# Forming the prepared FFN weights from pieces already loaded, a full-width bias matmul, a new order of the first FFN product and measured durations in the planner of a two-layer transformer kernel

## Chip, cores and metric

One Trainium2 chip; the kernel runs on one core. The metric is the device time of one execution in microseconds (us). The kernel before takes 1254.91 us (median of 6 runs, 1253.64 to 1258.09). All runs compared in this document are in the same (fast) state.

## The reference

Two identical layers, each a sliding dilated attention and a feed-forward network (FFN) with squared relu, both behind a layernorm and both with a residual. S = 2048 tokens, D = 1024, 32 heads, 8 taps at distance 2, F = 3584, weights in bf16.

Condensed (the reference writes it out at greater length):

```python
def _A_ref(x, wqkv, wo):                       # cut to what matters
    q, k, v = split_heads(x @ wqkv)            # 32 heads of 32
    idx = pos[:, None] - 2 * arange(8)         # 8 taps, dilation 2
    logits = einsum("bhsd,bhswd->bhsw", q, k[idx]) * scale   # masked where idx < 0
    return merge_heads(einsum("bhsw,bhswd->bhsd", softmax(logits), v[idx])) @ wo

def _B_ref(x, w1, b1, w2, b2):
    h = relu(x @ w1 + b1)
    return (h * h) @ w2 + b2

for layer in range(2):                         # written out in the reference
    x = x + _A_ref(_layernorm(x), wqkv, wo)
    x = x + _B_ref(_layernorm(x), w1, b1, w2, b2)
```

## The kernel before

The work is cut into 8 units (2 layers x 4 blocks of 512 tokens). The engines are named as in the profile: PE does the matmuls, DVE the elementwise work on tensors, ACT the activations and copies, POOL next to nothing here; SP issues most of the DMA transfers. A bank is one of eight buffers (`ps` in the program) that PE writes its sums to. A unit has these steps: layernorm and transposed input `xnA`; the q, k and v products (`pq`); the attention, whose products `P` and `pr` are formed on DVE and whose logits `lg` are summed by PE; the output projection `py`, the second layernorm and `xnB`; FFN product 1 (`ph` in unit 0; banks X, Y, Z in the others); FFN product 2 (banks X, Y, Z of the weights w2). Units 1 to 7 do both FFN products by a scheme of seven half-size products in place of eight, which needs sums and differences of pieces of w1 and w2. These are formed once, beside unit 0, and kept in DRAM as `w1s` and `tw`.

No order of instructions is written down: the program adds operations with an engine, a duration, a priority and buffers, and a planner written in Python simulates the engines and emits each engine's list in the order it finds.

```python
        while left:
            progress = False
            for e in engs:
                if efree[e] > t + 1e-9 or not ready[e]:
                    continue
                skipped = []
                picked = None
                while ready[e]:
                    item = heapq.heappop(ready[e])
                    o = item[2]
                    need = {}
                    ok = True
                    for b in o.bufs:
                        if b.slot is None:
                            need[b.cls] = need.get(b.cls, 0) + 1
                            if b.tag in self.caps and (live.get(b.tag, 0) >= self.caps[b.tag] or b.idx != placed.get(b.tag, 0)):
                                ok = False
                    if ok and all(len(free[c]) >= n for c, n in need.items()):
                        picked = o
                        break
                    skipped.append(item)
                    if len(skipped) > 40:
                        break
        # ... (cut)
            t, _, o, own = heapq.heappop(events)
            while True:
                if o is not None:
                    for s in o.succ:
                        if o.mb or (s.eng == o.eng) == own:
                            s.ndep -= 1
                            if s.ndep == 0:
                                heapq.heappush(ready[s.eng], (s.prio, seq, s)); seq += 1
        # ... (cut)
```

The bias of the second FFN product is a matmul with one row, put in front of the products of a bank:

```python
        self.b2r = const.tile([1, D], BF, name="b2r")
        nc.gpsimd.dma_start(self.b2r[:], self.b2.rearrange("(o d) -> o d", o=1))
        self.ones = const.tile([1, 128], BF, name="ones")
        nc.vector.memset(self.ones[:], 1.0)
# ... and in front of a bank's products (cut):
                    def fm(w=w, q=q, half=half):
                        if b2 is not None and half == 0:
                            nc.tensor.matmul(banks[q][:], self.ones[:], self.b2r[:, b2 * BLK:(b2 + 1) * BLK], start=start, stop=False,
                                             skip_group_check=True)
                        for j in range(g):
                            jj = half * g + j
```

The limits on live buffers by name, among them one transposed input `xnA` and one `tv` buffer:

```python
        p.caps.update(w=5, xt=2, P0=4, P1=4, pr=2, pb=2, dn=1, e=1, xm=6, xnA=1, xnB=1, xn=2, xo=2, q=1, k=1, v=1, o=1, r2=1, s1=1, tw=4, tv=1, T=1, wl=2)
```

The preparation loads w2 and w1 a second time:

```python
    def combine_group(self, j0, n):
        nc, p = self.nc, self.p
        step = 4
        b = {}
        for k2 in range(2):
            for n2 in range(2):
                t = b[k2, n2] = Buf("4K", "tw", [128, step, BLK], F16)
                self.dma(lambda t=t, n=n: t[:, :n].bitcast(BF), lambda k2=k2, n2=n2, j0=j0, n=n: self.w2_block(k2, n2)[:, j0:j0 + n, :],
                         (), [(t, 0)], n * 0.131, name="twl", lat=10.0)

        def comb(dst, a, asrc, c, csrc, i):
            def f():
                va = a[:, :n].bitcast(BF) if asrc else a[:, :n]
                vc = c[:, :n].bitcast(BF) if csrc else c[:, :n]
                nc.vector.tensor_tensor(dst[:, :n], va, vc, ALU.subtract)
            p.add("DVE", dve(n * BLK), f, [(a, 0), (c, 0)], [(dst, 0)], self.nxt(), name="tw")
            self.dma(lambda: self.tw[i][:, j0:j0 + n, :], lambda: dst[:, :n], [(dst, 0)], [(("tw", i), j0)], n * 0.131, prio=-10.0, name="tws")
        b11, b12, b21, b22 = b[0, 0], b[0, 1], b[1, 0], b[1, 1]
        comb(b11, b12, True, b11, True, 0)
        comb(b12, b22, True, b12, True, 2)
        comb(b22, b22, True, b11, False, 1)
        comb(b21, b21, True, b22, False, 3)
```

```python
    PAIR = [(0, 1), (1, 1), (0, 5), (1, 5), (0, 6), (1, 6), (0, 2), (0, 7), (1, 2), (1, 7), (0, 4), (0, 3), (1, 4), (1, 3)]
    LAST = [(0, 1), (0, 5), (0, 2), (0, 6), (0, 7), (0, 4), (0, 3)]

    def combine_w1_group(self, dp, after):
        nc, p = self.nc, self.p
        F2 = self.F // 2
        order = self.PAIR if dp // 2 * 2 + 1 < self.NDP else self.LAST
        dst = self.w1s[dp // 2]
        at = {pr: i for i, (d, pr) in enumerate(order) if d == dp % 2}

        def cell(i):
            return (("w1s", dp // 2), i)

        def raw(m2, k2):
            return self.w1_v[:, 4 * k2:4 * k2 + 4, m2 * F2 + dp * 256:m2 * F2 + (dp + 1) * 256]
        for pr, m2, k2 in ((1, 0, 0), (2, 0, 1), (4, 1, 1)):
            self.dma(lambda i=at[pr]: dst[:, i], lambda m2=m2, k2=k2: raw(m2, k2), (), [cell(at[pr])], 0.3, after=after, name="w1raw", cast=BF)
        t = Buf("8K", "tv", [128, 4, 1024], F16)
        for i, (m2, k2) in enumerate(((1, 1), (0, 0), (1, 0), (0, 1))):
            self.dma(lambda i=i: t[:, i].bitcast(BF).rearrange("p (k n) -> p k n", k=4), lambda m2=m2, k2=k2: raw(m2, k2), (), [(t, i)], 0.3, after=after, name="tvl", lat=12.0)

        def comb(o, a, araw, b, braw, op, pr):
            def f():
                va = t[:, a].bitcast(BF) if araw else t[:, a]
                vb = t[:, b].bitcast(BF) if braw else t[:, b]
                nc.vector.tensor_tensor(t[:, o], va, vb, op)
            p.add("DVE", dve(1024), f, [(t, a), (t, b)], [(t, o)], -50.0, name="tv")
            self.dma(lambda: dst[:, at[pr]].rearrange("p k n -> p (k n)"), lambda: t[:, o], [(t, o)], [cell(at[pr])], 0.26, prio=-10.0, name="tvs")
        comb(0, 2, True, 0, True, ALU.add, 5)
        comb(2, 1, True, 2, True, ALU.subtract, 7)
        comb(1, 0, False, 1, True, ALU.subtract, 6)
        comb(3, 3, True, 1, False, ALU.subtract, 3)
```

The first FFN product of units 1 to 7 takes the prepared weights in groups of up to four; product 1 leaves bank X, ACT copies X to `u`, and the next product in X waits for that copy:

```python
        for d0 in range(0, self.NDP, 2):
            order = self.PAIR if d0 + 1 < self.NDP else self.LAST
            steps = [self.ffn1_step(r2, d0 + i) for i in range(min(2, self.NDP - d0))]
            for j, (d, pr) in enumerate(order):
                if j % 4 == 0:
                    n = min(4, len(order) - j)
                    w = Buf("8K", "w", [128, 4, 4, 256], F16) if u + 1 < self.NU or j % 8 else Buf("8Q", "wl", [128, 4, 4, 256], F16)
                    self.dma(lambda w=w, n=n: w[:, 0:n], lambda d0=d0, j=j, n=n: self.w1s[d0 // 2][:, j:j + n],
                             [(("w1s", d0 // 2), j + i) for i in range(n)], [(w, 0)], n * 0.262,
                             after=[st["attended"]] if w.cls == "8Q" else (), name="w")
                steps[d](pr, w, j % 4, *rhs[pr])
# in ffn1_step, what follows each product (cut):
            if pr == 1:
                keep(1)
            elif pr == 2:
                vadd(r1, 0, 1, Y)
            elif pr == 6:
                keep(2)
            elif pr == 7:
                keep(3)
                vadd(r3, 1, 3, Z)
                for a in range(2):
                    vrelu(r3, a, 1, h + f0 + a)
            elif pr == 4:
                for a in range(2):
                    p.add("ACT", act(256), lambda a=a: nc.scalar.activation(out=r3[:, a, 0, :], in_=X[:, a, :], func=ACTF.Relu,
                                                                            bias=self.b1T[:, h + f0 + a:h + f0 + a + 1], scale=1.0),
                          [(X, 0)], [(r3, (a, 0))], 2.0, name="relu")
                square(r3, h + f0)
            elif pr == 3:
                vadd(r1, 1, 2, Z)
                for a in range(2):
                    vrelu(r1, a, None, f0 + a)
                square(r1, f0)
```

The order in which the program adds the steps:

```python
        for u in range(NU):
            if u + 1 < NU:
                self.SA(u + 1)
                if u == 0:
                    self.combine_w2()
                    self.SQ(u + 1, "kq")
                    self.SW(u)
                else:
                    self.SQ(u + 1, "k")
                    self.SW(u)
                    self.SQ(u + 1, "q")
                self.SQ(u + 1, "v")
                self.S2(u + 1, (1, 1) if u + 1 == NU - 1 else (3, 3))
            (self.SF1 if u else self.SF1_plain)(u)
            if u == 0:
                for dp in range(self.NDP):
                    pe = [o for o in self.p.ops if o.eng == "PE"]
                    self.combine_w1_group(dp, [pe[len(pe) * (dp + 3) // (self.NDP + 4)]])
            if u == NU - 2:
                self.SW(u + 1)
            self.SF2(u)
```

The softmax here doesn't subtract the row's maximum and nothing guards it: scores larger than these inputs give would overflow.

## Time and profile before

| quantity | value |
| --- | --- |
| time, median of 6 runs | 1254.91 us |
| span of the profiled execution | 1252.7 us |
| PE busy | 1193.9 us (95%) |
| bytes moved by DMA | 368.20 MB |
| start of unit 1's first FFN product | 302.95 us |
| start of the last 21 matmuls | 1244.47 us |

How to read the views. The page lists the busy time of each engine and slices the span into 40 parts, with the busy share in tenths. The list of waits has, for each engine and tile, the operation that ended the wait, then the total in us, the number of waits and the longest. The timeline has the start, the length, the engine, the line, the operation and, in brackets, the idle time before it and what ended it. The prediction shows most of these for the kernel before.

In the timeline, the start of unit 1's first FFN product and a bias matmul with its successor:

```profile
302.95 1.91 PE L785 MATMUL X<-xnB,w 128*128 128x256 f16 x16
...
1242.22 0.39 PE L836 MATMUL X<-b2r,ones 1*128 1x512 bf16 x1
1242.54 1.69 PE L840 MATMUL X<-w,r 128*128 128x512 f16 x7
```

The first line divides the run: what lies before it is called early, what lies between it and the last group of matmuls late. The bias matmul holds PE 0.32 us until the next one starts. And one row of the table by stretches, 40 to 80 us (columns: length; busy us and count of PE, PE's weight loads, DVE, ACT, POOL; granted clock of PE; DMA share; GB/s):

```profile
40.00:80.00 40.00, 27.76 (x128) 17.20 (x126) 37.12 (x47) 16.82 (x34) 0.00 (x0) 0.91 0.94 296
```

PE does 27.8 us of work in 40 while DVE and DMA are both nearly full.

### The profile page before, as it was taken

Reading aid. Unit: us, or ns where it says so; the run is one execution under the profiler, and the core shown is the slowest. Engines: PE = TensorE matmul, PEld = TensorE weight load, DVE = VectorE, ACT = ScalarE, POOL = GpSimd, SP = SyncE. Lnnn points to the kernel's source line nnn. Section 1 sums busy time; section 2 is a strip of 40 time slices with the busy share of each in tenths; the row PEclk is TensorE's granted clock in tenths of the full one; section 3 lists DMA queues with packets and bytes.
Section 4 is the critical chain, followed back from the end, with each engine's and each line's share of the span. In section 5 each row is a group of like instructions: output and inputs, shape, how many; then the busy total and the mean of one; then the engine's idle time right before and its main releaser. Section 6 shows DMA issues by size and latency. Waiting matters only on the chain.

```text
span 1252.7 us, 17924 instructions
## 1 busy us (share of the span) xinstructions
PE 1193.9 (95%) x6844; PEld 731.8 (58%) x6844; DVE 1035.2 (83%) x1555; ACT 674.2 (54%) x1240; POOL 4.0 (0%) x10
## 2 busy tenths in 40 slices
PE   6969989899999999999999999999999999999998
PEld 3635534357845578456864568545684557844853
DVE  5899979959989599986999779995999959997562
ACT  6624875059920798019970399406992174742630
POOL 1000000000000000000000000000000000000000
PEclk9989999999999999999999999999999999999999
DMA  9899999989999689995989779997799956788874
GB/s 314 303 288 305 351 350 306 361 294 280 316 341 336 203 277 319 346 319 186 350 315 334 284 233 372 299 311 252 235 337 367 318 167 221 254 285 304 290 267 166
DMA packets 240550, 368.20 MB, mean 294 GB/s; under 512 B 67664, under 2 KB 170576, under 8 KB 231504
## 3 DMA queue, kind: packets, MB, share of 16 engines
q1 hardware_dynamic: 229344, 353.41, 83.7%
q10 hardware_dynamic: 7488, 13.63, 2.9%
q0 software_dynamic: 3632, 0.02, 0.4%
q8 instruction: 53, 0.87, 0.3%
q14 instruction: 33, 0.27, 0.1%
HBM read 312.48 MB, written 46.40 MB: 286 GB/s over the span
## 4 chain that ended last, share of the span: by engine, by line
PE 57%; DVE 18%; ACT 12%; DMA 6%; SPq 3%; issue 2%; ACTq 1%; DVEq 0%
PE X L840 13%; PE X L785 10%; PE pq L557 8%; PE Z L840 7%; PE Z L785 6%; DVE P L589 5%; PE Y L840 4%; DVE P L597 4%; SPq L290 3%; DMA w<-in_B_w_dram 3%; ACT xn L410 3%; PE py L685 3%; ACT xn L439 3%; PE Y L785 2%; ACT xn L435 2%
## 5 line engine op out<-in xcount | busy, mean ns | idle before, releaser
L557 PE MATMUL pq<-xnA,w 128*128 128x512 f16 x1536 | 342.1, 383 | 19.2 <-DMA xnA<-xnd0A 12.0
L557 PEld LDWEIGHTS <-w 128*128 128x128 bf16 x1536 | 220.3, 144 | 136.8 <-issue 18.8
L785 PEld LDWEIGHTS <-w 128*128 128x128 f16 (+1 forms) x2520 | 246.4, 98 | 46.0 <-issue 11.2
L840 PEld LDWEIGHTS <-r 128*128 128x128 f16 x1344 | 128.7, 98 | 161.0 <-issue 9.3
L840 PE MATMUL X<-w,r 128*128 128x512 f16 (+1 forms) x896 | 201.8, 379 | 3.1 <-DMA w<-in_B_w_dram 3.1
L589 DVE TENSOR_TENSOR P<-q,k 128x2048 f16<-128x2048 f16 x128 | 151.7, 1224 | 56.5 <-ACT q L559 49.0
L559 ACT CAST k<-pq 128x512 f16<-128x512 f32 x64 | 37.4, 587 | 291.0 <-PE pq L557 290.0
L649 DVE TENSOR_TENSOR pr<-pb,v 128x2048 f16<-128x2048 f16 x128 | 156.4, 1222 | 0.2
L785 PE MATMUL X<-T,w 128*128 128x256 f16 x1120 | 136.5, 272 | 9.1 <-ACT u L759 8.9
L597 DVE TENSOR_TENSOR P<-P,P 128x2048 f16<-128x2048 f16 x99 | 120.9, 1222 | 2.2
L685 PE MATMUL py<-w,o 128*128 128x512 bf16 x512 | 112.3, 379 | 0.0
L773 ACT ACTIVATE r<-rr 128x1024 f16<-128x1024 f16 x98 | 101.5, 1058 | 13.1 <-DVE rr L769 11.8
L759 ACT CAST u<-X 128x512 f16<-128x512 f32 x147 | 84.5, 586 | 44.8 <-PE X L785 40.3
L652 DVE TENSOR_TENSOR pr<-pr 128x1024 f16<-128x1024 f16 x128 | 88.1, 689 | 2.7
L690 DVE TENSOR_TENSOR xm<-py,xt 128x512 f32<-128x512 f32 x64 | 43.9, 690 | 50.9 <-PE py L685 45.5
L685 PEld LDWEIGHTS <-o 128*128 128x128 bf16 x512 | 50.0, 98 | 59.8
L762 DVE TENSOR_TENSOR rr<-u,Z 128x512 f16<-128x512 f16 x98 | 65.4, 683 | 20.2 <-PE Z L785 11.1
L435 ACT ACTIVATE xn<-xm 128x1024 f16<-128x1024 f32 x32 | 33.9, 1060 | 58.9 <-DVE xm L690 58.0
L653 DVE TENSOR_TENSOR pr<-pr 128x512 f16<-128x512 f16 x128 | 54.4, 425 | 4.4
L840 PE MATMUL Y<-w,r 128*128 128x512 bf16 x224 | 51.9, 380 | 2.1 <-DMA w<-in_B_w_dram 2.1
L769 DVE TENSOR_SCALAR rr<-rr,b1T 128x256 f16<-128x256 f16 (+1 forms) x196 | 51.3, 315 | 1.3
L840 PE MATMUL Z<-w,s 128*128 128x512 f16 x224 | 51.3, 380 | 0.0
(92 smaller groups left out, 1261.5 us busy)
## 6 DMA issues: line engine op xcount, KB each, us to landing
w<-w1s SPq DMA_DIRECT2D x63, 1024.0 KB, 7.9
w<-tw SPq DMA_DIRECT2D x64, 896.0 KB, 7.6
w<-in_A_wqkv_dram SPq DMA_DIRECT2D x48, 1024.0 KB, 9.2
w<-in_B_w_dram SPq DMA_DIRECT2D x48, 896.0 KB, 8.2
w<-in_A_wo_dram SPq DMA_DIRECT2D x16, 1024.0 KB, 9.1
xt<-xs SPq DMA_DIRECT2D x32, 512.0 KB, 9.3
w<-w1s SPq DMA_DIRECT2D x21, 512.0 KB, 9.2
xs<-xo SPq DMA_DIRECT2D x32, 256.0 KB, 6.2
```

What stands on the lines that cost most here:

```text
L435: nc.scalar.activation(out=xn[:], in_=xv(), func=ACTF.Identity, accum_out=s1())
L557: nc.tensor.matmul(pq[:], wv[:, kd % 4, c0:D:8], xnT[:, :, kd, :], start=(kd == 0), stop=(kd == KD - 1))
L589: nc.vector.tensor_tensor(cur[:], q[:, c, None, hb * HB:(hb + 1) * HB].to_broadcast([128, W, HB]), _win_ap(k[:, c, :], HALO + hb * HB, HB) ...
L597: nc.vector.tensor_tensor(other[:], other[:], cur[:], ALU.add)
L649: nc.vector.tensor_tensor(pr[:], pb[:], _win_ap(v[:, c, :], HALO + hb * HB, HB), ALU.mult)
L652: nc.vector.tensor_tensor(pr[:, 0:4, :], pr[:, 0:4, :], pr[:, 4:8, :], ALU.add)
L685: nc.tensor.matmul(py[:], o[:, c, tl * 128:(tl + 1) * 128], wos[db][:, c, :], start=(c == 0), stop=(c == NCH - 1))
L759: p.add("ACT", act(512), lambda: nc.scalar.copy(us[i][:], X[:]), [(X, 0)], [(us[i], 0)], 1.0, name="u")
L762: p.add("DVE", dve(512, False), lambda: nc.vector.tensor_tensor(r[:, :, m, :], us[i][:], bank[:], ALU.add), [(us[i], 0), (bank, 0)], [(r, ...
L773: p.add("ACT", act(1024), lambda: nc.scalar.activation(out=r2[:, f:f + 2, :].rearrange("p a t -> p (a t)"), in_=r[:].rearrange("p a m t -> ...
L785: nc.tensor.matmul(bank[:, a, :], lw[:, k, a * 128:(a + 1) * 128], rhs(k), start=(start and k == 0 and a == 0), stop=(k == 3), skip_group_ ...
L840: nc.tensor.matmul(banks[q][:], left(jj, q), w[:, j, :], start=(start and jj == 0 and b2 is None), stop=(jj == h - 1), skip_group_check=True)
```

## The change

Its intent is to have less DMA and DVE work beside unit 0, where PE has its holes, and plans that are truer to the chip. Five parts are told apart below:

1. Preparation: w1 and w2 combinations are formed from the pieces that unit 0's own products have loaded (`keep_w1`, `keep_w2`); uncombined w1 pieces are copied from DRAM to DRAM; unit 0's second FFN product becomes plain (eight products); two `xnA` buffers, six small `tv` buffers.
2. The bias by a full 128-row matmul (a matrix with ones in row 0).
3. A new order of the seven products in FFN product 1, with weights in chunks of 4.
4. Planner: 0.3 us of slack ahead of PE operations that wait for another engine, a longer look-ahead, durations as measured.
5. wo loaded in other halves.

The diff, cut to its core:

```diff
@@ -21,6 +22,7 @@
 
 MM = 0.2157
 LAT = 0.25
+PE_SLACK = 0.3
 DMA_LAT = 2.2
 DMA_MBS = 0.36
 
@@ -138,7 +140,7 @@
                         picked = o
                         break
                     skipped.append(item)
-                    if len(skipped) > 40:
+                    if len(skipped) > 300:
                         break
                 for it in skipped:
                     heapq.heappush(ready[e], it)
@@ -169,12 +171,19 @@
                 raise RuntimeError(f"plan is stuck at {t}: {stuck} live {live} free { {c: len(f) for c, f in free.items()} }")
             t, _, o, own = heapq.heappop(events)
             while True:
-                if o is not None:
+                if own is None:
+                    heapq.heappush(ready[o.eng], (o.prio, seq, o)); seq += 1
+                elif o is not None:
                     for s in o.succ:
                         if o.mb or (s.eng == o.eng) == own:
                             s.ndep -= 1
-                            if s.ndep == 0:
-                                heapq.heappush(ready[s.eng], (s.prio, seq, s)); seq += 1
+                            if s.ndep:
+                                continue
+                            if s.eng == "PE" and o.eng != "PE":
+                                heapq.heappush(events, (t + PE_SLACK, seq, s, None))
+                            else:
+                                heapq.heappush(ready[s.eng], (s.prio, seq, s))
+                            seq += 1
                     if not own:
                         for b in o.bufs:
                             b.left -= 1
@@ bias (cut) @@
@@ -242,10 +251,12 @@
         self.b1T = const.tile([128, KF], F32, name="b1T")
         with nc.allow_non_contiguous_dma(reason="tiny bias load"):
             nc.gpsimd.dma_start(self.b1T[:], self.b1.rearrange("(c p) -> p c", p=128))
-        self.b2r = const.tile([1, D], BF, name="b2r")
-        nc.gpsimd.dma_start(self.b2r[:], self.b2.rearrange("(o d) -> o d", o=1))
-        self.ones = const.tile([1, 128], BF, name="ones")
-        nc.vector.memset(self.ones[:], 1.0)
+        self.b2r = const.tile([128, D], BF, name="b2r")
+        nc.gpsimd.dma_start(self.b2r[:], self.b2.rearrange("(o d) -> o d", o=1).to_broadcast((128, D)))
+        self.row0 = const.tile([128, 128], F16, name="row0")
+        nc.vector.memset(self.row0[:], 1.0)
+        nc.gpsimd.affine_select(out=self.row0[:], in_=self.row0[:], pattern=[[0, 128]], compare_op=ALU.is_equal,
+                                fill=0.0, base=0, channel_multiplier=1)
 
         self.wqkv_v = self.wqkv.rearrange("(kt p) n -> p kt n", p=128)
         self.wo_v = self.wo.rearrange("(p c) n -> p c n", c=self.NCH)
+    def add_b2(self, bank, n2, start):
+        self.nc.tensor.matmul(bank[:], self.row0[:], self.b2r[:, n2 * BLK:(n2 + 1) * BLK], start=start, stop=False, skip_group_check=True)
@@ buffers (cut) @@
-        p.caps.update(w=5, xt=2, P0=4, P1=4, pr=2, pb=2, dn=1, e=1, xm=6, xnA=1, xnB=1, xn=2, xo=2, q=1, k=1, v=1, o=1, r2=1, s1=1, tw=4, tv=1, T=1, wl=2)
+        p.caps.update(w=5, xt=2, P0=4, P1=4, pr=2, pb=2, dn=1, e=1, xm=6, xnA=2, xnB=1, xn=2, xo=2, q=1, k=1, v=1, o=1, r2=1, s1=1, tv=6, T=1, wl=2)
@@ preparation of w2; combine_w2 and combine_group are removed, SF2_plain is added (cut) @@
+    def keep_w2(self, j0, n, w):
+        nc, p = self.nc, self.p
+        t = [Buf("2K", "tv", [128, 2, BLK], F16) for _ in range(4)]
+
+        def raw(k2, n2):
+            return w[:, k2, :n, n2 * BLK:(n2 + 1) * BLK]
+
+        def comb(i, a, b, r):
+            p.add("DVE", dve(n * BLK), lambda: nc.vector.tensor_tensor(t[i][:, :n], a(), b(), ALU.subtract), r, [(t[i], 0)], 45.0, name="tv")
+            self.dma(lambda: self.tw[i][:, j0:j0 + n, :], lambda: t[i][:, :n], [(t[i], 0)], [(("tw", i), j0)], n * 0.13, prio=50.0, name="twst", lat=8.0)
+        comb(0, lambda: raw(0, 1), lambda: raw(0, 0), [(w, 0)])
+        comb(1, lambda: raw(1, 1), lambda: t[0][:, :n], [(w, 1), (t[0], 0)])
+        comb(2, lambda: raw(1, 1), lambda: raw(0, 1), [(w, 0), (w, 1)])
+        comb(3, lambda: raw(1, 0), lambda: t[1][:, :n], [(w, 1), (t[1], 0)])
@@ order of FFN product 1 and copies of raw w1 pieces; keep_w1 forms the four combinations as keep_w2 does (cut) @@
+    def ffn1_order(self):
+        out = [(0, 1), (1, 1)]
+        for a in range(0, self.NDP, 2):
+            steps = [d for d in (a, a + 1) if d < self.NDP]
+            then = [(d, 1) for d in (a + 2, a + 3) if d < self.NDP]
+            for pr in (5, 6, 2, 7):
+                out += [(d, pr) for d in steps]
+            out += then
+            for pr in (4, 3):
+                out += [(d, pr) for d in steps]
+        return out
+
+    def copy_w1(self, after):
+        after = iter(after)
+        for i, (dp, pr) in enumerate(self.order1):
+            if pr in (1, 2, 4):
+                gate = next(after)
+                m, k = {1: (0, 0), 2: (0, 1), 4: (1, 1)}[pr]
+                c0 = m * (self.F // 2) + dp * 256
+                self.dma(lambda i=i: self.w1s[i // 4][:, i % 4], lambda k=k, c0=c0: self.w1_v[:, 4 * k:4 * k + 4, c0:c0 + 256],
+                         (), [(("w1s", i // 4), i % 4)], 0.3, prio=1e5 + i, after=[gate], name="w1cp", cast=BF)
@@ durations (cut) @@
-            p.add("ACT", 1.3, f1, xr, [(xn, 0), (sm, 0)], prio, name="ln1")
-            p.add("ACT", 1.3, f2, xr + [(sm, 0)], [(xn, 0), (sm, 1)], prio - 0.1, name="ln2")
-            p.add("ACT", 0.5, f2b, [(sm, 0), (sm, 1)], [(sm, 1)], prio - 0.15, name="ln2b")
+            p.add("ACT", 1.47, f1, xr, [(xn, 0), (sm, 0)], prio, name="ln1")
+            p.add("ACT", 1.35, f2, xr + [(sm, 0)], [(xn, 0), (sm, 1)], prio - 0.1, name="ln2")
+            p.add("ACT", 0.8, f2b, [(sm, 0), (sm, 1)], [(sm, 1)], prio - 0.15, name="ln2b")
-            p.add("DVE", 0.15 + len(ms) * 0.067, lambda: nc.vector.tensor_scalar(out=v(), in0=v(), scalar1=self.b1T[:, f:f + 1], scalar2=0.0,
+            p.add("DVE", 0.21 + len(ms) * 0.07, lambda: nc.vector.tensor_scalar(out=v(), in0=v(), scalar1=self.b1T[:, f:f + 1], scalar2=0.0,
-                    p.add("ACT", act(256), lambda a=a: nc.scalar.activation(out=r3[:, a, 0, :], in_=X[:, a, :], func=ACTF.Relu,
+                    p.add("ACT", 0.48, lambda a=a: nc.scalar.activation(out=r3[:, a, 0, :], in_=X[:, a, :], func=ACTF.Relu,
@@ wo (cut) @@
-        wos = [self.weights(self.wo_v[:, :, g * 512:(g + 1) * 512], KD) for g in range(D // 512)]
+        wos = [self.weights(self.wo_v[:, 4 * g:4 * g + 4, :], KD, wide=True) for g in range(2)]
@@ build (cut) @@
-                    self.combine_w2()
-                    self.SQ(u + 1, "kq")
+                    self.run(self.SQ(u + 1, "kq"))
                     self.SW(u)
+                    self.copy_w1([op for op in self.p.ops if op.eng == "PE" and op.name in ("pq", "py")][-24:])
+                    self.run(self.SF1_plain(u), self.SQ(u + 1, "v"))
                 else:
-                    self.SQ(u + 1, "k")
+                    self.run(self.SQ(u + 1, "k"))
                     self.SW(u)
-                    self.SQ(u + 1, "q")
-                self.SQ(u + 1, "v")
+                    self.run(self.SQ(u + 1, "q"))
+                    self.run(self.SQ(u + 1, "v"))
                 self.S2(u + 1, (1, 1) if u + 1 == NU - 1 else (3, 3))
-            (self.SF1 if u else self.SF1_plain)(u)
-            if u == 0:
-                for dp in range(self.NDP):
-                    pe = [o for o in self.p.ops if o.eng == "PE"]
-                    self.combine_w1_group(dp, [pe[len(pe) * (dp + 3) // (self.NDP + 4)]])
+            if u:
+                self.SF1(u)
             if u == NU - 2:
                 self.SW(u + 1)
-            self.SF2(u)
+            (self.SF2 if u else self.SF2_plain)(u)
```

## The prediction

> **What bounds the kernel now.** I read the page first (busy shares, slices), then PE's waits, then PE's timeline around its gaps, then the groups of instructions and the DMA issues.
>
> The busy shares and the slices, from the page:
>
> ```profile
> PE 1193.9 (95%) x6844; PEld 731.8 (58%) x6844; DVE 1035.2 (83%) x1555; ACT 674.2 (54%) x1240; POOL 4.0 (0%) x10
> ...
> PE   6969989899999999999999999999999999999998
> ...
> PEclk9989999999999999999999999999999999999999
> DMA  9899999989999689995989779997799956788874
> ```
>
> PE (the matmul engine) is the bound. Its holes and its only slow clock lie in the first eight slices of 31 us; after that it is nine tenths or more. DMA is at its limit in those slices too. So the question for every part is what it does to PE's idle time early, and to PE's own work later. PE's waits say who caused the holes:
>
> ```profile
> PE pq L557 <- DMA xnA<-xnd0A: 12.0, 1, 12.0
> PE lg L604 <- DVE P L597: 9.3, 7, 4.8
> PE pt L493 <- ACT xn L479: 9.1, 3, 8.1
> PE X L785 <- ACT u L759: 8.9, 10, 1.8
> PE pq L557 <- DMA w<-in_A_wqkv_dram: 6.0, 3, 3.7
> PE X L840 <- DMA w<-in_B_w_dram: 3.1, 2, 1.8
> ```
>
> The third is the start of the program and stays. The largest early ones in PE's timeline (start, us, ..., in brackets the idle time before):
>
> ```profile
> 64.44 3.62 PE L557 MATMUL pq<-xnA,w 128*128 128x512 f16 x16
> 80.10 29.13 PE L557 MATMUL pq<-xnA,w 128*128 128x512 f16 x128 [12.05 <-DMA xnA<-xnd0A]
> 109.07 7.07 PE L685 MATMUL py<-w,o 128*128 128x512 bf16 x32
> ...
> 182.53 1.89 PE L604 MATMUL lg<-P,grp 128*128 128x512 f16 x4 [4.76 <-DVE P L597]
> 184.21 12.75 PE L711 MATMUL ph<-xnB,w 128*128 128x512 f16 x56
> ...
> 247.06 14.61 PE L557 MATMUL pq<-xnA,w 128*128 128x512 f16 x60 [3.73 <-DMA w<-in_A_wqkv_dram]
> ```
>
> From this I take the unit of all the sums. A stream of full matmuls starts one every 0.2157 us (in the last unit the timeline has 56 of them from 1224.00 to 1236.08: 12.08 / 56). After the 12.05 us hole the 128 take 28.97 us (80.10 to 109.07) instead of 27.6: the slow clock costs 1.4 more. The same after the other two: about 1.3 after 182.53, 1.5 after 247.06 (60 in 14.45 instead of 12.94).
>
> **What the Trainium skill says.** "TensorE: Matmul & The Clock Gate", section "What's actually happening", gives 512 / 2.4 GHz + 2.5 ns = 215.7 ns for a warm matmul of 512 columns, and a half-rate clock after a window of some 3.4 us idle. The trace agrees: 0.2157 us, and a mean granted clock of 0.84 in the stretch with the 12 us hole. "TensorEngine Tiling (Array Packing)", section "Key Properties", says that switching the tiling mode drains the engine. That bears on the bias matmul of one row (its form is 1*128): in the timeline 28 matmuls start at 1236.08, so its slot is at 1242.12; it starts at 1242.22 and the next one at 1242.54, 0.20 us later than slot and length allow; whether a drain is the reason, no view shows. "VectorE: DVE Perf Modes", section "The perf-mode tier table", has 1224 ns for a tensor_tensor of 2048 16-bit elements; here the product rows of the attention have 1222 to 1224 ns, so the DVE work moved below can be summed from its rows.
>
> **The change part by part.**
>
> (1) Preparing the weights. Before, the first unit reads w1 and w2 for its own products and both again to form the sums and differences (the fast seven-product scheme) that later units use:
>
> ```profile
> tv<-in_B_w_dram SPq DMA_DIRECT2D x28, 256.0 KB, 7.7
> ...
> tw<-in_B_w_dram SPq DMA_DIRECT2D x12, 512.0 KB, 9.4
> ...
> tw<-in_B_w_dram SPq DMA_DIRECT2D x4, 256.0 KB, 6.5
> ```
>
> After, the combinations are formed from the w1 and w2 already loaded. That removes 28 x 0.25 = 7 MB and 12 x 0.5 + 4 x 0.25 = 7 MB. The first unit's second FFN product becomes plain: it reads w2 once (7 MB) instead of 14 pieces of 0.875 (12.25 MB): 5.25 less. Together 19 MB, at the page's mean of 294 GB/s an estimated 65 us of all DMA engines, out of about 280 us. The DVE work of combining stays (4 x 7 of 0.69, and the same elements for w2), but none of it now precedes the first unit's attention: 6 of 1.22 and 8 of 0.69, 13 us, leave DVE's way there. The order of the built program confirms it: the transposes of the second unit's input move from after 47 transfers of the DMA queue to places 13 to 19, beside the attention of unit 0; in before they are issued at 69.9 us, 25 us after their last input was stored (44.9). They will be there long before PE asks at 68. So the 12.05 and its 1.4 go. The wait of 4.76 on DVE goes too: DVE itself lost 6.83 us there waiting for a slot that a store of a combination held (tw<-tw), and that store is gone. The 3.73 + 0.45 on query/key weights at 242 to 247 with their 1.5 should go with the DMA load. Sum: 12.05 + 1.4 + 4.76 + 1.3 + 4.18 + 1.5 = 25.2 us.
>
> (2) The plain product costs PE 4 x 2 x 28 + 8 bias = 232 matmuls where the fast one has 7 x 2 x 14 + 6 = 202: 30 x 0.2157 = 6.5 us, less 6 x 0.2 for its old bias matmuls: +5.3. On DVE it takes 10 of 1.08 and 6 of 0.69, 15 us, away.
>
> (3) What is not won of (1). Without the hole PE would be at py at 96 instead of 109. Its second half needs all of unit 0's attention, which DVE ended at 121.3. DVE's work up to there falls by 13 us, but it was waiting for q part of the time, so it gains some 4.5 us until the exponentials, and 3 more after (5.3 less of combining, 2.4 more of moved-up products): about 114. PE gets there after 96 + 6.9 (py) + 10.4 (48 of the v product) + 1.0 = 114: balanced. Then the last two layernorms on ACT (4.9 us each, one after the other) end about 10 us after py, as before (130.3 to 140.5), but only 16 of the v product are left to fill it: 5 us idle and about 1.5 us slow clock. The v weights are loaded only when q's are free, at 96, behind 15 copies of w1: I allow 2 us. Sum 8.5 given back; net of (1) to (3): 25.2 - 5.3 - 8.5 = 11.4 us.
>
> (4) The bias by a full 128-row matmul: 42 in the seven other units, each 0.20 us shorter: 8.4 us, all of it PE time with nothing beside it.
>
> (5) The new order of the first FFN product puts other products between the one that ACT must copy out and the one that adds to the same bank, also in the last, single step (plain pieces of the next product stand in between): most of the 8.9 us goes, I take 7. The slack of 0.3 us in the planner, and the ACT and DVE durations now as measured, should make lg wait less: 4.5 us of its 9.3 lie after 303 us, I take 3. The waits for w2 and w1 weights there (3.1 + 2.1 + 1.6) I leave.
>
> (6) wo loaded in other halves: the same bytes, longer rows, no PE time; but now the first py needs both halves.
>
> Sum: 11.4 + 8.4 + 10 = 29.8 us, rounded to 31 with a little for the less crowded queue at the start (1.85 us of PE's wait for weights at 22.5). Predicted 1224 us, 2.5% less.
>
> **The rivals.** First, the w1/w2 preparation is bound by DVE and the DMA queue, not by DMA bytes. Speaking for it: DVE is at 0.9 and more of most early slices, the program's order puts the loads of the next unit's weights behind stores that wait for DVE, and only 8 transfers can be out at a time. By my sum DVE ends unit 1's attention at about 247 where PE wants it at 251: 4 us of room. Against it: 15 us less DVE work. If it holds, half of the 25 us comes back as other waits, and the time is 1235 to 1240. Second, the early gain is whole (layernorm and v weights hidden) and the waits of (5) all go: 1210 to 1214. Third, DMA is not relieved because the copies of w1 come in a burst of 21 between 68 and 113 us and hold up wo, v and w1: they are 5.25 MB beside 8 MB of needed loads in 45 us, an estimated 294 GB/s, just what the page shows as its mean; a few us, 1228 to 1232. Fourth, the new order asks for banks that the logits also need: new PE waits in each of seven units at 1 us each cancel (5): 1232.
>
> **Range and chances.** The bias part is nearly sure (8), the early part lies between 5 and 20, the later waits between 2 and 14. That gives 1212 to 1238 eight times in ten. The 2% line is at 1229.8; the middle lies 6 us on the good side of it: faster by over 2% 0.70, within 2% 0.28, slower 0.02.
>
> **What would show it.** Right: no PE wait on the transposes; first FFN product of unit 0 starting near 130 instead of 140.5; unit 1's first FFN product starting near 291 instead of 303; bias matmuls at 0.216 spacing; PE matmul count 6874; PE's wait on ACT's copies near 2. Wrong: a clock under 0.95 anywhere between 60 and 250; new PE waits for v or wo weights or for DVE's products over 8 us in all; steady units that do not get at least 2 us shorter than their 148 (397.2 to 545.0 in the chain of waits).

A correction to a citation in it: the 215.7 ns of a warm matmul of 512 columns stands in the Trainium skill, page "TensorE: Matmul & The Clock Gate", in the section "Wait — 56ns, not 53.3ns?"; the section named there has the half-rate clock and its window of some 3.4 us.

## More of the kernel before

In the groups of instructions (line, engine, operation, output <- inputs, count, busy us, mean ns of one, idle before), two short operations of the FFN:

```profile
L801 ACT ACTIVATE rr<-X,b1T 128x256 f16<-128x256 f32 x98 | 41.5, 475 | 12.0 <-PE X L785 11.9
L769 DVE TENSOR_SCALAR rr<-rr,b1T 128x256 f16<-128x256 f16 x98 | 22.3, 281 | 0.5
```

The planner believes 395 ns (`act(256)`) and 217 ns for these two: a plan that keeps ACT and DVE just in time is late on the chip.

## The result, and the profile after

The changed kernel takes 1229.29 us (median of 8 runs, 1226.28 to 1230.63); the kernel before, run beside it, 1255.15 us (16 runs, 1251.18 to 1258.09). The ratio is 0.9794, with a 95% interval of 0.9781 to 0.9808: 25.9 us less by the medians. That it is faster is clear of noise; whether by more than 2% is not, as the interval reaches over 0.98. The result is correct.

The page after:

```profile
PE 1188.5 (97%) x6874; PEld 740.1 (60%) x6874; DVE 1024.2 (83%) x1553; ACT 679.5 (55%) x1240; POOL 4.3 (0%) x11
...
PE   6999899999999999999999999999999999999998
PEclk9999899999999999999999999999999999999999
DMA  9686999889798697978989699995989855688964
```

PE has 30 matmuls more, as worked out in the prediction, and a smaller busy time. The holes in the third, sixth and eighth slices are gone; one dent and one slow clock are left at the fifth. DMA moved 348.29 MB, 19.9 less (predicted 19). PE's largest waits:

```profile
PE pt L533 <- ACT xn L519: 9.3, 3, 8.2
PE lg L645 <- DVE P L638: 6.2, 4, 2.5
PE pt L533 <- ACT xn L450: 4.4, 2, 4.1
PE Z L367 <- DVE xo L941: 2.8, 2, 1.4
...
PE X L833 <- ACT u L807: 1.3, 1, 1.3
```

The wait of 12.0 for `xnA` is not there, nor the 8.9 for ACT's copies `u` (1.3 left). New are waits for DVE's output additions `xo`. The timeline at the places that the prediction named:

```profile
60.38 34.70 PE L597 MATMUL pq<-xnA,w 128*128 128x512 f16 x160
94.92 7.07 PE L726 MATMUL py<-w,o 128*128 128x512 bf16 x32
...
131.94 13.07 PE L757 MATMUL ph<-xnB,w 128*128 128x512 f16 x48 [1.68 <-DVE xnB L536]
...
289.88 1.91 PE L833 MATMUL X<-xnB,w 128*128 128x256 f16 x16
...
1218.00 0.38 PE L367 MATMUL X<-b2r,row 128*128 128x512 bf16 x1
1218.22 1.67 PE L887 MATMUL X<-w,r 128*128 128x512 f16 x7
```

160 matmuls run in one piece through the place of the 12 us hole. Unit 0's first FFN product starts at 131.94 (140.49 before), unit 1's at 289.88 (302.95). The bias matmul holds PE 0.22 us instead of 0.32. The row of the stretch from 40 to 80 us:

```profile
40.00:80.00 40.00, 39.79 (x185) 25.43 (x184) 33.93 (x45) 17.21 (x32) 0.00 (x0) 1.00 0.75 227
```

PE does 39.8 us of work in the 40, with DMA at 0.75 instead of 0.94.

The 24.5 us between the two profiled executions divide: the early part is 302.95 - 289.88 = 13.1 us shorter, the late part 941.5 - 930.1 = 11.4 us (1244.47 - 302.95 against 1219.94 - 289.88).

### The profile page after: what moved, and what is told of

Its sections match the earlier page's. It is cut to its first block, busy times and chain, and to the rows that moved or that the text cites. A ratio compares the mean times of both kernels' runs of the same rounds, so it can differ in the third digit from the quotient of the medians.

```text
span 1228.2 us, 17991 instructions
## 1 busy us (share of the span) xinstructions
PE 1188.5 (97%) x6874; PEld 740.1 (60%) x6874; DVE 1024.2 (83%) x1553; ACT 679.5 (55%) x1240; POOL 4.3 (0%) x11
## 2 busy tenths in 40 slices
DMA packets 209239, 348.29 MB, mean 284 GB/s; under 512 B 67136, under 2 KB 133952, under 8 KB 196352
## 4 chain that ended last, share of the span: by engine, by line
PE 82%; DVE 10%; DMA 4%; ACT 2%; issue 1%; SPq 0%; ACTq 0%; DVEq 0%
PE pq L597 20%; PE X L833 14%; PE X L887 12%; PE py L726 7%; PE Z L833 7%; PE Z L887 6%; PE ph L757 4%; PE py L358 4%; PE Y L833 3%; DMA w<-in_B_w_dram 3%; PE Y L887 2%; DVE pr L690 2%; PE lg L645 2%; DMA w<-in_A_wqkv_dram 1%; DVE P L630 1%; DVE pr L693 1%
## 5 line engine op out<-in xcount | busy, mean ns | idle before, releaser
L833 PEld LDWEIGHTS <-w 128*128 128x128 f16 (+1 forms) x2544 | 248.9, 98 | 36.5 <-issue 1.5
L887 PEld LDWEIGHTS <-r 128*128 128x128 f16 x1176 | 114.7, 98 | 143.1 <-issue 5.8
L887 PE MATMUL X<-w,r 128*128 128x512 f16 (+1 forms) x784 | 177.1, 379 | 2.3 <-DVE xo L941 1.3
L833 PE MATMUL X<-T,w 128*128 128x256 f16 x1104 | 133.9, 273 | 1.3 <-ACT u L807 1.3
L821 ACT ACTIVATE r<-rr 128x1024 f16<-128x1024 f16 x98 | 102.1, 1057 | 11.4 <-DVE rr L817 8.7
L675 ACT ACTIVATE dn<-dn 128x256 f32<-128x256 f32 x16 | 6.6, 415 | 178.9 <-DVE dn L672 178.9
L757 PE MATMUL ph<-xnB,w 128*128 128x512 f16 x224 | 51.4, 393 | 1.7 <-DVE xnB L536 1.7
```

The source lines that it names most:

```text
L757: nc.tensor.matmul(ph[:], w[:, m, kd, a * 128:(a + 1) * 128], xnT[:, :, kd, :], start=(kd == 0), stop=(kd == KD - 1))
L821: p.add("ACT", act(1024), lambda: nc.scalar.activation(out=r2[:, f:f + 2, :].rearrange("p a t -> p (a t)"), in_=r[:].rearrange("p a m t -> ...
L833: nc.tensor.matmul(bank[:, a, :], lw[:, k, a * 128:(a + 1) * 128], rhs(k), start=(start and k == 0 and a == 0), stop=(k == 3), skip_group_ ...
L887: nc.tensor.matmul(banks[q][:], left(jj, q), w[:, j, :], start=(start and jj == 0 and b2 is None), stop=(jj == h - 1), skip_group_check=True)
```

## The experiments

Theory after the result: the early 13 us come from the preparation (part 1), some 8 of the late 11 from the bias (part 2), the rest from parts 3 and 4, of which the order takes the waits on ACT's copies away. Rivals: the early gain comes from the second `xnA` buffer alone; the waits on ACT go by the durations or the slack, not the order. Twelve kernels were run. In names, b_ is the kernel before with something added, a_ the changed kernel with something taken back. Start is that of unit 1's first FFN product, late the time from there to the last group of matmuls, both in the profiled execution. These two columns come from one execution each, and executions of one kernel differ: the 16 of the kernel before span 7 us, and its mean clock was 0.987 to 0.992 in the rounds of b_bias. The profiled executions of b_xna2 and b_planner were 3.1 us faster than the medians of their kernels, that of b_dur 2.5 us slower. So 2 to 3 us in one of these columns, without the median, show little.

| kernel | median, us | ratio to before [95%] | start, us | late, us |
| --- | --- | --- | --- | --- |
| before | 1254.91 | 1 | 302.95 | 941.5 |
| changed | 1229.29 | 0.9794 [0.9781, 0.9808] | 289.88 | 930.1 |
| b_bias | 1248.43 | 0.9946 [0.9929, 0.9963] | 304.78 | 933.6 |
| b_xna2 | 1254.99 | 0.9994 [0.9975, 1.0014] | 303.60 | 938.3 |
| b_order | 1262.69 | 1.0057 [1.0040, 1.0073] | 313.79 | 939.6 |
| b_dur | 1265.70 | 1.0078 [1.0050, 1.0106] | 305.61 | 952.6 |
| b_planner | 1259.48 | 1.0046 [1.0029, 1.0063] | 310.46 | 936.0 |
| b_nodve (wrong) | 1250.10 | 0.9965 [0.9940, 0.9990] | 298.15 | 939.9 |
| a_preponly | 1240.40 | 0.9884 [0.9869, 0.9898] | 290.41 | 940.0 |
| a_onerow | 1236.78 | 0.9854 [0.9841, 0.9866] | 291.53 | 937.3 |
| a_xna1 | 1228.62 | 0.9785 [0.9767, 0.9803] | 292.71 | 926.5 |
| a_oldorder | 1245.58 | 0.9919 [0.9906, 0.9932] | 289.88 | 945.7 |
| a_slack0 | 1233.20 | 0.9821 [0.9808, 0.9834] | 291.10 | 932.9 |
| a_tvlate | 1228.92 | 0.9801 [0.9778, 0.9823] | 291.16 | 926.7 |

### b_bias and a_onerow: the bias matmul alone, both ways

b_bias is the kernel before with the full-row bias; a_onerow is the changed kernel with the one-row bias. In both, all orders stay as they were (the traces have the same instructions in the same order).

```diff
-        self.b2r = const.tile([1, D], BF, name="b2r")
+        self.b2r = const.tile([128, D], BF, name="b2r")      # b2 in every row
-        self.ones = const.tile([1, 128], BF, name="ones")
+        self.row0 = const.tile([128, 128], F16, name="row0") # ones in row 0, else 0
```

> The kernel before with only the bias matmuls changed (128-row weight with ones in row 0, bias copied to 128 partitions); the order of all engines stays the same instruction for instruction. Theory (the one-row matmul costs 0.20 us of PE time too much, nothing beside it): 48 x 0.20 = 9.6 us less, 1245.5 us, 0.8% faster; the bias matmuls at 0.216 us spacing. Rival (the extra 0.2 us is hidden, as PE waits for others later anyway): no change within 2 us.

> The changed kernel with the one-row bias of before; orders of all engines unchanged. 50 bias matmuls x 0.20 us = 10 us more if all count: 1239 us. In the kernel before the same part alone gave 6.8 us of an expected 9.6, with 7.9 of 8.4 in the stretch after 303 us. Theory (all count, because PE is the bound all along): 8 to 10 us. Rival (part is hidden by PE waiting less elsewhere): under 6 us.

Measured: the late part falls by 7.9 us in the kernel before (941.5 to 933.6) and rises by 7.2 us in the changed one (930.1 to 937.3). Over the 42 bias matmuls of the seven units this is 0.19 and 0.17 us each; the timeline had said 0.20. The time moves by 6.9 us (medians 1255.31 of the kernel before in those rounds, and 1248.43) and by 7.5 us. In b_bias the early part lost 1.8 us, at a slower mean clock of the span (0.989 against 0.993); PE's waits up to there are nearly the same (34.0 us, 34.3 before), the clock is not (0.96, 0.97 before), so this is a difference between two executions and not the bias. Part 2 is settled: 7 to 8 us, all late. Both forecasts of the whole time (9.6 us, and 8 to 10) were too high: they also count the bias matmuls of unit 0, whose part does not show in the early stage.

### b_xna2 and a_xna1: the second input buffer alone, both ways

```diff
-xnA=1,
+xnA=2,
```

> The kernel before with two buffers instead of one for the transposed input of the attention block; all preparation traffic of w1 and w2 stays. Rival theory (the 12.05 us hole was a wait for the single buffer, which PE's v product of unit 0 frees only at 68 us, plus four transposes issued one after the other): the hole and its 1.4 us of slow clock go, 11 to 14 us less, about 1242 us. My recorded theory (crowding of the DMA queue by the w1 and w2 preparation delayed the transposes): the hole stays above 6 us, or comes back as other waits for weights, less than 6 us gained.

> The changed kernel with one buffer instead of two for the transposed input. Rival theory (single buffer): a PE wait on the transposes of 9 to 12 us and a slow clock after it come back, 1239 to 1243 us. Recorded theory (queue crowding): the queue is free of preparation traffic now, so the transposes are short; wait under 6 us, 1229 to 1235 us.

With a second buffer in the kernel before, the 12 us hole is gone, and py starts at 101.50 instead of 109.07, but unit 1's FFN starts at 303.60: all of it is given back. The timeline of b_xna2 shows to what:

```profile
51.18 1.02 PE L604 MATMUL lg<-P,grp 128*128 128x512 f16 x4 [1.89 <-DVE P L589]
...
57.20 2.16 PE L604 MATMUL lg<-P,grp 128*128 128x512 f16 x8 [1.54 <-DVE P L589]
...
101.50 7.07 PE L685 MATMUL py<-w,o 128*128 128x512 bf16 x32
...
222.85 5.55 PE L840 MATMUL X<-w,r 128*128 128x512 f16 x14 [5.57 <-DMA w<-tw]
```

Small waits on DVE's products before py, waits of 3.4 and 3.7 us on the layernorm of ACT at 136 and 141, and 5.6 us for a prepared piece of w2, whose load was issued at 215.84 behind three stores of such pieces. In the changed kernel with one buffer again, no wait on the transposes comes back, and the time is the same (1228.62, interval 0.9767 to 0.9803); 7.3 us of waits on DVE's attention output before py are new there. With one buffer the transposes of unit 1 can only start when unit 0 no longer reads it. In the kernel before its v product read it until 68.06, and they were issued at 69.93; in a_xna1, at 52.90. So the hole took both, one buffer and the old plan around it: either change alone removes it. Yet the second buffer is not what gains: whoever closes only the hole finds the stage held by something else.

### b_nodve: what holds the early stage

b_xna2 once more, without the 44 DVE operations that form the sums; the pieces are stored as loaded and later read as plain weights. The loads, stores and bytes stay. Its output is wrong, which doesn't matter for the time.

```diff
-            p.add("DVE", dve(n * BLK), f, [(a, 0), (c, 0)], [(dst, 0)], self.nxt(), name="tw")
-            p.add("DVE", dve(1024), f, [(t, a), (t, b)], [(t, o)], -50.0, name="tv")
-            start, raw = pr in (1, 2, 5), pr in (1, 2, 4)
+            start, raw = pr in (1, 2, 5), True
```

> Wrong result on purpose. The kernel before with the second input buffer (as in b_xna2, which gained nothing), and the 44 DVE subtractions and additions that form the sums of w1 and w2 left out: the pieces are stored as they were loaded, so the loads, the stores and their bytes are all as in b_xna2, and the later products read them as plain weights. Theory: in b_xna2 the 12 us hole went, but the stage is bound by DVE (attention plus 37 us of combining), so all came back as waits on DVE. Then with the combining gone PE's waits on DVE products and ACT layernorms before 250 us shrink, unit 1's first FFN product starts at 285 to 293 instead of 303.6, and the time is about 1240 to 1246. Rival: the stage is bound by the DMA queue and its bytes (19 MB more than in the changed kernel): unit 1's first FFN product stays at 299 or later and the time at 1250 or more.

Measured: 298.15, so 5.5 us better than b_xna2 (4.9 by the medians). It lies between the two theories (285 to 293 and 299 or later), and so does the time, 1250.10: neither holds as stated. Of DVE's 249 us of work up to 300 us some 29 were taken away (248.6 to 220.0), but the wait chain is now another. PE's and DVE's waits (DVE's between 35 and 125 us):

```profile
PE lg L602 <- DVE P L587: 5.7, 4, 2.8
...
DVE P L587 <- ACT q L557: 10.7, 4, 4.9
```

PE waits for DVE's products, DVE for ACT's copy of q, and that for PE's q product (ACT's wait, 13.0 us between 35 and 125): a circle through three engines that a plan must fill with other PE work, and this plan has only 131 matmuls between 40 and 80 us where the changed kernel has 185. The DMA share is 1.09, 1.08 and 1.07 in the three stretches of 40 us from 40 to 160, in the changed kernel 0.75 and 0.74 in the first two of them and 1.13 in the third. So taking DVE's combining away, with the waits of the stores on it, is worth some 5 us of the 13. Less than half of it is shorter waiting: PE's waits up to unit 1's FFN are 33.2 us in b_xna2 and 31.3 in b_nodve; the rest is clock (0.97 and 0.99 up to there). That the bytes are the other part fits the shares, but no run took the bytes away alone, so it is not shown.

### a_preponly: the preparation alone

The changed kernel with the old bias, the old order, slack 0, the old durations and wo in the old halves. The new planner times of unit 1's transposes stay too. The look-ahead stays at 300: with 40 the planner stops, stuck, and builds no kernel. Its list holds 183 transfers where it stops; the first ones can't be placed yet, and the 21 copies of w1, which have the lowest priority, are the last 21, out of reach of a look-ahead of 40. The look-ahead by itself is no rival: the kernel before, built with 300, is the same program to the byte (a build, no run).

```diff
-PE_SLACK = 0.3
+PE_SLACK = 0.0
-            p.add("ACT", 1.47, f1, xr, [(xn, 0), (sm, 0)], prio, name="ln1")
+            p.add("ACT", 1.3, f1, xr, [(xn, 0), (sm, 0)], prio, name="ln1")
+    PAIR = [(0, 1), (1, 1), (0, 5), (1, 5), (0, 6), (1, 6), (0, 2), (0, 7), (1, 2), (1, 7), (0, 4), (0, 3), (1, 4), (1, 3)]
... (cut: the rest as in the diff of the change, backwards)
```

> Of the change only the preparation part (combinations from the loaded w1 and w2, plain product in unit 0, two input buffers, interleaving, early marks) and the planner's longer look-ahead, without which its plan gets stuck; one-row bias, old product order, no slack, old durations and old wo halves. Theory (the early part alone is worth about 12 us): about 1243 us, unit 1's first FFN product at about 291 us, and the waits after it about as before (20 us, with 8 to 9 on ACT's copies). Rival (without the planner's slack and durations the early gain is lost in new waits): 1250 us or more.

Measured: start 290.41, 12.5 of the 13.1 us, and a late part of 940.0, 1.5 us shorter than before. The time is 1240.40, ratio 0.9884. The waits on ACT's copies are 5.8 us, not the 8 to 9 expected. All seven kernels that have the new preparation start unit 1's FFN between 289.9 and 292.7; all that have the old one between 298.2 and 313.8. The early gain belongs to part 1, whatever the planner, the order and the number of buffers.

### b_order, b_dur and b_planner: parts 3 and 4 on the kernel before

b_order has the new order and the chunks of 4 alone. b_dur has only the two FFN durations as measured. b_planner has order, durations, slack and look-ahead together.

```diff
-                    p.add("ACT", act(256), lambda a=a: ...relu of 256 columns      # b_dur, b_planner
+                    p.add("ACT", 0.48, lambda a=a: ...
-            p.add("DVE", 0.15 + len(ms) * 0.067, ...bias and relu                  # b_dur, b_planner
+            p.add("DVE", 0.21 + len(ms) * 0.07, ...
-        for d0 in range(0, self.NDP, 2):                                           # b_order, b_planner
+        for j, (d, pr) in enumerate(self.order1):
+PE_SLACK = 0.3                                                                     # b_planner
```

> The kernel before with only the new order of the first FFN product's seven products (and the prepared w1 stored in that order). Theory: PE's waits on ACT's copies fall from 8.9 to about 2 us, 5 to 8 us less, about 1249 us. Rival (banks held longer by the pulled-ahead first products give new PE waits on DVE, as seen in the changed kernel with 5.0 us on the output adds): gain under 3 us, with waits on DVE's output adds appearing in this run too.

> The kernel before with only two planner durations of the first FFN product changed to what the trace measures: the 256-column relu on ACT 0.40 to 0.48 us, the DVE bias-and-relu 0.22 to 0.28 and 0.28 to 0.35 us. Old order of products, slack 0, everything else old. Theory from the runs so far (the order alone left PE's waits on ACT's copies at 8.3 us, the old order inside the changed kernel has 2.0): it is the durations that removed these waits. Then they fall from 8.9 us to 1 to 3, the time from the first FFN product of unit 1 to the last matmuls from 941.5 to about 935, the time to about 1249 (ratio about 0.995). Rival (the prediction's step 5: the order does it, or the slack): they stay at 7 to 9 us and the time within 2 us of before.

> The kernel before with the whole of the prediction's step 5 and nothing else: the new order of the first FFN product with its weights in chunks of 4, the slack of 0.3 us, the look-ahead of 300 and the measured durations of ACT, DVE and the late loads. Weight preparation, bias matmul, buffers and wo stay old. Each alone did not help (order 1.006, the two FFN durations 1.008). First theory: the planner's part is worth what is left when the ratios of the other two are taken out of the changed kernel's (0.9794 / 0.9884 / 0.9946 = 0.996): the parts work together and add up, PE's waits on ACT's copies fall under 2.5 us, the time from unit 1's first FFN product to the last matmuls is 941.5 to about 937, the time about 1250. Second theory: the planner's part gains only after the preparation is taken out of the way (it makes the plan's early stage true to the chip): ratio 1.00 or above, with new early waits of PE on weights and transposes, though the waits on ACT's copies after unit 1's start fall all the same. Rival three: the waits on ACT's copies stay above 5 us; then none of order, durations and slack removes them, and the prediction's reason for step 5 is wrong altogether.

Each of the three makes the kernel before slower, by 0.5 to 0.8%. The order alone leaves PE's waits on ACT's copies at 8.3 us, against 8.9, so its theory fell. Its rival named the wrong place: no waits on DVE's output additions came, the loss is early (a hole of 14.7 us, a start 10.8 us later). The durations alone leave them at 7.2 and bring new ones; the first theory of b_dur fell. PE's waits of b_dur from its start of unit 1's FFN on:

```profile
PE X L785 <- ACT u L759: 7.2, 12, 1.1
PE Y L840 <- DMA w<-in_B_w_dram: 6.8, 4, 2.7
PE X L840 <- DMA w<-in_B_w_dram: 3.6, 2, 2.0
```

All together, in b_planner, they fall to 3.7, and the late part becomes 5.6 us shorter (936.0); but unit 1's FFN starts 7.5 us later than before:

```profile
PE pq L576 <- DMA xnA<-xnd0A: 15.2, 1, 15.2
PE lg L623 <- DVE P L616: 10.4, 2, 8.8
...
PE X L804 <- ACT u L778: 3.7, 4, 1.2
```

The hole is 15.2 us instead of 12.0, and a wait of 8.8 us for DVE's products stands where 4.8 stood. So the second theory of b_planner held for the sum (ratio 1.0046), with early waits on transposes and DVE's products, and the first for the length of the late part (936.0, expected 937), though not for ACT's waits (3.7, expected under 2.5). The profiled execution was the fastest of its six, so the late gain may be smaller. With the old preparation what the planner's part gains late it pays early.

### a_oldorder and a_slack0: parts 3 and 4 taken back from the changed kernel

```diff
# a_oldorder (cut); PAIR and LAST are those of the kernel before
-        out = [(0, 1), (1, 1)]
+        out = []
+            out += [(a + d, pr) for d, pr in (self.PAIR if a + 1 < self.NDP else self.LAST)]
# a_slack0
-PE_SLACK = 0.3
+PE_SLACK = 0.0
```

> The changed kernel with the old order of the seven products. Theory of the prediction (the order removes the waits on ACT's copies): ACT waits back to 7 to 9 us, 5 to 7 us slower, 1235 us. Rival (after the order alone in the kernel before took nothing off the ACT waits, 8.3 us: it is the planner's slack and durations that put other work between): ACT waits stay under 3 us, time within 3 us of the changed kernel's.

> The changed kernel with the planner's slack for PE at 0 instead of 0.3 us. Rival of the last run (slack): ACT waits go up to 6 us or more and waits on DVE's products too, 5 to 8 us slower, 1236 us. Prediction's theory (the order does it): ACT waits stay under 3 us; only the logits' waits on DVE go up, 1 to 3 us slower.

Measured: without the new order 1245.58, 16 us more, and the late part is 15.6 us longer. Yet the waits on ACT's copies are only 2.0 us there. What stands there instead are waits for w2 weights (7.2 + 1.5 + 0.6) and for DVE (3.3 + 2.6 + 1.4), beside 6.0 of the logits as in the changed kernel (6.2): 24.9 us in all against 16.8. So neither expectation held: ACT's waits stayed small, as the rival had it, but the time did not stay. The other half is the clock. In the timeline and the table by stretches of a_oldorder:

```profile
445.91 2.98 PE L830 MATMUL Z<-T,w 128*128 128x256 f16 x16 [2.55 <-DVE T L430]
...
446.00:449.00 3.00, 3.00 (x18) 2.25 (x18) 2.93 (x6) 1.47 (x4) 0.00 (x0) 0.60 1.04 349
449.00:452.00 3.00, 3.00 (x25) 2.49 (x24) 2.97 (x4) 1.60 (x3) 0.00 (x0) 0.83 1.07 426
```

After a wait of 2.55 us the granted clock is 0.60 for 3 us and 0.83 for the next 3: 3 x 0.40 + 3 x 0.17 = 1.7 us lost besides the wait. Four more such places (after waits of 2.2, 3.3 and 2.5 us, and after three of 0.7, 1.3 and 1.5 in a row) make 10.5 us of the late part of a_oldorder; the changed kernel has 2.1. I summed this as (1 - granted clock) x 10 us over stretches of 10 us, the last ones reaching past the last group. The 0.6, 0.7 and 1.5 of before, b_planner and a_preponly are rests of this rounding: their late parts have no slow clock. With it the late parts add up to within 1.2 us:

| kernel | PE's waits, late | clock lost, late | sum | sum against its base | late part against its base |
| --- | --- | --- | --- | --- | --- |
| before | 20.5 | 0.6 | 21.1 | base | base |
| b_order | 16.8 | 1.7 | 18.5 | -2.6 | -1.9 |
| b_dur | 25.4 | 6.9 | 32.3 | +11.2 | +11.1 |
| b_planner | 15.4 | 0.7 | 16.1 | -5.0 | -5.6 |
| a_preponly | 19.3 | 1.5 | 20.8 | -0.3 | -1.5 |
| changed | 16.8 | 2.1 | 18.9 | base | base |
| a_oldorder | 24.9 | 10.5 | 35.4 | +16.5 | +15.6 |
| a_slack0 | 16.6 | 5.2 | 21.8 | +2.9 | +2.8 |

The slack of 0.3 us is worth some 3 to 4 us, nearly all through the clock: without it the waits are the same 16.6 us, with one longer piece (logits 3.2 at the longest instead of 2.5), which a slow clock follows. But about half of the clock's difference comes after a wait of 2.51 us that both kernels have: in the changed kernel it ends at 1016.75 and costs 1.7 us of clock, in a_slack0 it ends at 1020.47 and the slow clock lasts twice as long. That half is not the slack's doing. As for the waits on ACT's copies: with the new preparation they are 5.8 us with none of order, durations and slack (a_preponly), 0.9 without slack, 2.0 without the order, 1.3 with all. With the old preparation they are 8.9 with none, 8.3 with the order alone, 7.2 with the two durations alone, 3.7 with all. So pairs remove most of them where single ones hardly do, but the pairs ran only with the new preparation. Order with slack and old durations was not run.

### a_tvlate: the last dent of the early part

In the changed kernel a w1 sum on DVE, waiting for its load, stands ahead of the last copy of `xnB`. Here the sums must come after all four copies.

```diff
# cut at ...; late is [(xnT, i) for i in range(4)]
-            p.add("DVE", dve(1024), lambda: ..., r, [(t, 0)], 95.0, name="tv")
+            p.add("DVE", dve(1024), lambda: ..., r + late, [(t, 0)], 95.0, name="tv")
```

> The changed kernel, with the forming of the w1 sums on DVE made to come after all four copies of unit 0's second layernorm output. In the changed kernel a sum that waits for a w1 load (landing 128.5 us) stands in DVE's order ahead of the last of these copies, and PE's first FFN product of unit 0 waits 1.68 us for it at 131.9, with a slow clock after it. Theory (DVE's order is what holds it): that wait goes, the first FFN product starts at 129 to 130.5, unit 1's first FFN product at 287 to 289 instead of 289.9, time about 1227. Rival: the product needs the same w1 load anyway and only the name of the wait changes, or the sums that come later hold up the stores: no gain, 1228 to 1232.

```profile
130.91 1.04 PE L533 MATMUL pt<-ident,xn 128*128 128x128 f16 x8 [4.09 <-ACT xn L450]
133.21 9.62 PE L757 MATMUL ph<-xnB,w 128*128 128x512 f16 x32 [1.25 <-DVE xnB L536]
```

The rival was right: the wait only shrinks from 1.68 to 1.25, behind the same 4.09 us for ACT's layernorm, and the product starts at 133.21, not earlier. The time, 1228.92, is that of the changed kernel. No version of mine beats the changed kernel by more than the runs scatter; a_xna1 and a_tvlate have late parts shorter by some 3.5 us and starts 1.3 to 2.8 us later.

## Why the prediction was right or wrong

The steps are numbered here as the prediction numbers them; its (1) to (3) are part 1 of the change, (4) is part 2, (5) parts 3 and 4, (6) part 5.

**Verdict and size.** Faster was right, and 1229.29 lies within the range; -25.9 us instead of -31. "By over 2%" fits the ratio 0.9794 but is not shown, as its interval (0.9781 to 0.9808) reaches over 0.98. The middle, 1224, was 5 us too low, mainly because step (5) brought 3.9 us where 10 had been predicted.

**Step (1), the preparation, with (2) and (3), its price.** Predicted -11.4 us net, measured -13.1 (a_preponly alone -12.5). The named waits are gone: the 12 us on `xnA`, the 4.76 on DVE, the 3.73 on weights. PE's 30 matmuls more are there. What was to be given back is there too: 4.09 us on the layernorm and 1.68 on `xnB`, with a slow clock after them (a mean of 0.66 between 130 and 140 us, so one of the prediction's signs of being wrong, a clock under 0.95 between 60 and 250, came although its price had been counted in). The reason given for the hole, the queue order, was not complete: it took the single buffer as well (unit 0 read it until 68.06 us), since either change alone removes it (b_xna2, a_xna1), and taking the hole away was worth nothing while the rest of the preparation stood. The first rival, a bound by DVE and the queue that would give half back, did not come in the changed kernel, but it describes the kernel before: there b_xna2 gave all of it back.

**Step (4), the bias.** Predicted -8.4, measured -7.9 and +7.2. Right; 0.17 to 0.19 us each instead of 0.20.

**Step (5), order and planner: the mis-sized term.** Predicted -10: 7 from ACT's copies because of the order, 3 from the logits. ACT's waits did fall by 7.6 us, but the late part apart from the bias fell only by 11.4 - 7.5 = 3.9 us. The logits' waits after unit 1's FFN start rose from 4.5 to 6.2 instead of falling by 3, and 5.0 us of new waits on DVE's outputs (`xo` 2.8 and 1.3, `xm` 0.9) came. This is the fourth rival's kind of loss, at other tiles than it named. The reason was wrong as well: the order alone removes hardly any of ACT's waits (8.3 of 8.9 left), nor do the two durations alone (7.2). The order is worth much all the same, 15.6 us in the changed kernel, through waits on weights and DVE and the slow clock they bring. The prediction had a sign of this in its own test: steady units were to get at least 2 us shorter. From one unit's last bias matmul to the next one's they went from 148.1 us (392.17 to 984.40, four units) to 146.6 (374.81 to 961.03), 1.5 us, of which six bias matmuls at 0.18 to 0.19 make 1.1: that sign of being wrong came.

**The rounding.** The steps summed to 29.8 and were rounded up to 31 for a less crowded queue at the start; that wait only went from 1.85 to 1.55 us.

**Step (6), wo.** Not tried by itself; a_preponly has the old halves and nearly all of the early gain. Third rival, the burst of copies: the DMA share from 40 to 120 us is 0.74 to 0.75; no sign of it there.

What stays open: the sums of parts do not add up to better than 3 to 4 us (late: b_planner -5.6, bias -7.2 to -7.9, a_preponly -1.5 make -14.3 to -15.0, where the changed kernel has -11.4), because each edit of the plan makes the planner deal all later waits anew, and perhaps by the scatter of single executions. And how the early gain divides between DMA bytes and the order of loads is not shown.

## What to carry to other kernels

When a hole has a nearest cause (one buffer), ask what would be met next if it went: here the second buffer closed the hole in the kernel before and gained nothing, and the changed kernel is as fast without it; the preparation around it had to change. Where a planner makes the order, a part of a change can't be priced by the waits that it is meant to remove: run it alone on the old kernel and taken back from the new one, since the two can differ: the new order cost 7 us in the old kernel and was worth 16 in the new one. And count a PE wait of more than 2 us together with the slow clock that may follow it: here 1.7 us more.

## What the Trainium skill lacked or had wrong

- Page "TensorE: Matmul & The Clock Gate", section "Why this matters for your kernels", asks for no idle gaps over some 3 us between bursts of matmuls. In these runs shorter ones were enough: after single waits of 2.2 us (337.40 us of a_oldorder) and 2.55 us (445.91), and after three of 0.67, 1.34 and 1.46 us within 6 us (1086.6 to 1092.2), the granted clock of a stretch of 10 us was 0.83 to 0.87; after one of 2.90 us (492.30) it stayed at 1.00. The row's limit by the length of one gap does not describe this. Each drop is a piece of 3.4 us at a granted clock of 0.50 (337.35 to 340.75) and cost 1.7 us; after the wait that ends at 1027.97 it was twice as long.
- Page "TensorEngine Tiling (Array Packing)", section "Key Properties", says that a mode switch drains the engine but not what that costs. A one-row matmul in a stream of full ones cost 0.17 to 0.19 us more than a full-row one (7.2 and 7.9 us over 42); that a drain is the reason, no run shows.
